# The values product of windowed attention split into quarters of the array

## The chip, the cores and the metric

The kernel runs on one core of one Trainium2 chip. The metric is the time of one execution on the device, in microseconds (us). TensorE does the matrix products, VectorE (DVE) and ScalarE (ACT) work on elements, GpSimd (POOL) does a few small things, SyncE (SP) issues the transfers.

## The reference

Three layers in a row, all in float32, for 4 sequences of 576 tokens, 8 heads of 64 (512 features):

```python
scores = scale * q @ k.T + slopes * -(pos_q - pos_k)      # per head
mask = (rel >= 0) & (rel < 128)                           # causal, a window of 128
attn = softmax(where(mask, scores, -1e9)) ;  x = attn @ v # 2304 x 512
h = x @ w_in ;  x = (h * clip(h + 3, 0, 6) / 6) @ w_out   # 512 -> 2048 -> 512
xn = x / rms(x) * rms_g
out = (silu(xn @ w_gate) * (xn @ w_val)) @ w_out2         # 512 -> 1536 -> 512
```

The window makes the attention local: a query tile of 128 sees keys of its own chunk of 128 and of the chunk before. In its own chunk query i sees keys 0 to i, in the one before it sees keys i+1 to 127.

## The kernel before

The 2304 tokens are 18 tiles of 128, in six blocks of three. Attention works on pairs of heads: for each block four pairs, 24 in all, and a pair has three steps, one for each query tile. The first feed-forward layer runs block by block; its inner loop (L710) has a slot for each of the 16 chunks of the hidden features. Work of the attention of the next block is laid into these slots by a table of offsets (L448 to L462), all in one program order that is written out by hand; each engine goes through its own instructions strictly in that order.

In every slot TensorE does product1 (L496, 12 matmuls into the one bank `ps_h`) and product2 of the slot before (L509, 9 matmuls). On `ps_h` ScalarE does the add-and-relu (L734), VectorE the min-and-multiply (L735), ScalarE the high part of the result (`g`, L744), VectorE the rest (L755). The next slot's product1 writes the same bank, so it waits for L735.

From the tenth pair on (`JOINT = 9`), a pair spreads over slots like this, pairs following each other every four slots:

- the scores slot: the scores of all three steps (L359, on quarters of the array), bias and maximum (L373, L380), exponentials (L388);
- the next slot: the divisions (L397, six on ScalarE) by the sums that POOL made. In the same slot stand the values of the pair before, so it is called the values slot here;
- the turn slot: VectorE transposes 32x32 blocks (L403), SyncE stores them to DRAM (L408);
- the fetch slot: SyncE loads them back in transposed order (L322);
- the next pair's scores slot: POOL selects what belongs to the chunk and to the one before (L423), into `pt`, 128 keys by two chunks by two heads by 128 queries. What the mask excludes is zero there;
- the next pair's values slot: the values product (L434).

The values product of a step is four matmuls of 128 keys by 64 features on 128 queries, for two chunks (`c`) and two heads (`a`), summed over the chunks in the bank `ps_av` (`sums_bank`). The first tile of a sequence that begins on a tile's edge has no chunk before it (`from_ = 1`) and takes two. Then `finish` (L327) moves the sum for all three steps to `xs`, the input of product1 one block later: ScalarE casts the high part (L335), VectorE subtracts for the low part (L336). After it SyncE is asked for the v of the pair after next (L310, two buffers).

In most slots of blocks three to five a unit of the second layer's weights is converted too (`W2.turn`, L219): L143, L133, L140 and at times L147 on VectorE, L136 and at times L145 on ScalarE, with loads (L203) and stores (L216) on SyncE.

The bank `ps_t` (`turned_bank`) takes transposes in the first nine pairs; later it only holds, with `ps_av`, the scores of the third step.

Of the kernel before, what the change touches and what calls it, by code (L numbers as in the profile page):

```python
# [11 lines left out]
F32R = mybir.dt.float32r  # L12
# [8 lines left out]
P = 128  # L21
B, H, S, D = 4, 8, 576, 64
# [3 lines left out]
KC = DM // P  # L26
# [20 lines left out]
JOINT = 9  # L47
# [21 lines left out]
def f32(ap):  # L69
    return ap.bitcast(F32)  # L70
# [3 lines left out]
def fused_kernel(ctx: ExitStack, tc: tile.TileContext, qd, kd, v, w1, w2, rms_g, out):  # L74
# [7 lines left out]
    vec, act, pool, pe, sp = nc.vector, nc.scalar, nc.gpsimd, nc.tensor, nc.sync  # L82
# [3 lines left out]
    xpool = ctx.enter_context(tc.tile_pool(name="xpool", bufs=2))  # L86
# [63 lines left out]
    def room(k, shape, dtype, name):  # L150
        return wpool.tile(shape, dtype, tag=f"w{k}", name=name)

    class First:
# [3 lines left out]
        def __init__(self):  # L157
            self.raw = [room(k, [P, 2 * DM], U64, "wraw") for k in range(M1)]
            self.loaded, self.runs, self.tiles = 0, [], []

        def load(self, upto):
            while self.loaded < min(upto, M1):
                sp.dma_start(out=self.raw[self.loaded], in_=w1[self.loaded])
                self.loaded += 1
# [116 lines left out]
    xs_of = {}  # L281
# [3 lines left out]
    turned_bank = ps_a.tile([P, 2, 2, P], F32, tag="T", name="ps_t")  # L285
# [3 lines left out]
    class Pair:  # L289


        def __init__(self, b, j):
            self.b, self.j = b, j
            self.i0, self.n = BLOCKS[b]
            self.lo = max(self.i0 - 1, 0)
            self.nch = self.i0 + self.n - self.lo
            self.acc = None
            self.plain = b * H // 2 + j in PLAIN

        def load(self):  # L300
            j, q0, nq, k0, nk = self.j, self.i0 * P, self.n * P, self.lo * P, self.nch * P
# [17 lines left out]
        def fetch(self):  # L319

            for k in range(0, P, 32):
                sp.dma_start(  # L322
                    out=weights_[k : k + 32, 1].rearrange("r u a (b s) -> r (u a b) s", s=32),
                    in_=self.d[:, :, :, k : k + 32].rearrange("u a (b r) s -> r (u a b) s", r=32),
                )

        def finish(self):  # L327

            nq = self.n * P
            x = self.acc.rearrange("p u q -> p (u q)")[:, :nq]  # L330
            if self.j == 0:
                xs = (x0pool if self.b == 0 else xpool).tile([P, KC, 2, 3 * P], F32R, tag="xs", name="xs")
                xs_of[self.b] = [xs[:, c] for c in range(KC)]
            t = xs_of[self.b][self.j]
            act.copy(t[:, 0, :nq], x)  # L335
            vec.tensor_sub(t[:, 1, :nq], x, f32(t[:, 0, :nq]))  # L336

    class Step:
# [89 lines left out]
        def values(self):  # L428
            pr = self.pair
            if pr.acc is None:  # L430
                pr.acc = sums_bank[:, :3]
            for c in range(self.from_, 2):
                for a in range(2):
                    pe.matmul(  # L434
                        pr.acc[a * D : (a + 1) * D, self.u],
                        lhsT=pr.vr[:, self.i - 1 + c - pr.lo, a * D : (a + 1) * D],
                        rhs=self.pt[:, c, a],
                        start=(c == self.from_),
                        stop=(c == 1),
                        skip_group_check=True,  # L440
                    )
# [8 lines left out]
    for k, pr in enumerate(pairs):  # L450
        b, j = divmod(k, H // 2)
# [12 lines left out]
    def at(t):  # L464
        return [slots[kind].get(t, []) for kind in KINDS]
# [8 lines left out]
                pairs[k].load()  # L474

    def finish(pr):
        pr.finish()
        k = pairs.index(pr) + 2
        if k < len(pairs):
            pairs[k].load_v()  # L480
# [108 lines left out]
    for t in range(AHEAD):  # L589
        q, s_, d_, t_, _, v_, _, _, _ = at(t)  # L590
# [46 lines left out]
    class Inputs:  # L637
# [19 lines left out]
        def sum(self, which, on, out):  # L657
            setattr(self, which, out)
            x, sub = self.block, on.tensor_sub
            if which == "S1":  # L660
                on.tensor_add(out, x(1, 0), x(1, 1))
            elif which == "S2":
                sub(out, self.S1, x(0, 0))
            elif which == "S3":
                sub(out, x(0, 0), x(1, 0))
            else:
                sub(out, x(0, 1), self.S2)
# [27 lines left out]
    for p, (b, m0, m1) in enumerate(PARTS):  # L695
        n = BLOCKS[b][1]
        last = p == len(PARTS) - 1
        nq = n * P
# [10 lines left out]
        xs = xs_of[b]  # L709
        for m in range(m0, m1):  # L710
            t, slot = slot, slot + 1
            q, s_, d_, t_, l_, v_, p_, r_, w_ = at(t)
# [37 lines left out]
                if m + 1 < CUT:  # L750
                    W1.step(m + 1, 3)
            for x in v_:
                if x.last:
                    finish(x.pair)
            vec.tensor_sub(g[:, 1, :nq], r[:, :nq], f32(g[:, 0, :nq]))  # L755
            for x in s_[2:]:
                x.bias()
            for x in s_:
# [13 lines left out]
                finish1(go)  # L772
            for x in l_:
                x.transpose()
            for x in d_:
                if x.via:
                    x.divide()
# [56 lines left out]
    acc = room(SUMS[0], [P, 4, DM], F32, "y"), room(SUMS[1], [P, 2, DM], F32, "y")  # L834
    acc = [acc[t // 4][:, t % 4] for t in range(6)]
# [29 lines left out]
    def group(i):  # L865
# [42 lines left out]
        if i + 3 not in ring and i + 3 not in parts:  # L908
            fetch(i + 3)
# [134 lines left out]
```

## Time and profile before

| | us |
|---|---|
| median of 3 runs | 930.15 (929.33 to 930.58) |
| the profiled execution | 929.06, of it the span 927.4 |
| TensorE busy | 912.2 (98% of the span) |
| VectorE busy | 634.8 (68%) |
| ScalarE busy | 456.0 (49%) |
| POOL busy | 181.6 (20%) |

The span runs from the first to the last instruction. Attention and first layer take its first 500 us or so, the second layer the rest. A matmul's end is modelled, so TensorE's busy time is no measure of how well it is used; starts are better. Every idle time of another engine is harmless unless TensorE waits behind it.

### The profile page before, as it was taken

How to read it: one execution, taken by the hardware profiler on the slowest of the kernel's cores; microseconds unless marked ns; L12 is line 12 of the kernel's file. 1: busy time of each engine (PE TensorE's matmuls, PEld its weight loads, DVE VectorE, ACT ScalarE, POOL GpSimd, SP SyncE). 2: the span in 40 equal slices, each digit the busy share in tenths (PEclk: the TensorE clock that was granted, in tenths of full speed). 3: DMA queues.
4: the chain of work that ended last, by engine and by line, in shares of the span. 5: the costliest groups of instructions: out<-in, count | busy, mean ns of one | idle time of the engine just before them, and what ended most of it. 6: DMA issues, size and time to landing. Idle time of an engine off the chain costs nothing.

```text
span 927.4 us, 15033 instructions
## 1 busy us (share of the span) xinstructions
PE 912.2 (98%) x5384; PEld 811.0 (87%) x5384; DVE 634.8 (68%) x1282; ACT 456.0 (49%) x994; POOL 181.6 (20%) x327
## 2 busy tenths in 40 slices
PE   7899999999999999999999999999999999999998
PEld 4588888888888888888999999999999999999997
DVE  5799666556887777886577667787545577545555
ACT  6899566565657656655455453423232223231120
POOL 4332013232234322332243322200000000000000
PEclk9999999999999999999999999999999999999999
DMA  7456412346998888884565788685757555755521
GB/s 241 173 212 224 168 40 67 77 86 186 257 276 236 221 226 227 206 211 116 158 216 220 270 263 309 244 288 204 276 207 276 209 204 205 276 209 209 209 88 68
DMA packets 156522, 186.84 MB, mean 201 GB/s; under 512 B 90528, under 2 KB 129952, under 8 KB 152096
## 3 DMA queue, kind: packets, MB, share of 16 engines
q1 hardware_dynamic: 156448, 185.89, 62.2%
q8 instruction: 42, 0.69, 0.3%
q14 instruction: 32, 0.26, 0.1%
HBM read 135.92 MB, written 49.94 MB: 200 GB/s over the span
## 4 chain that ended last, share of the span: by engine, by line
PE 94%; DVE 2%; ACT 2%; issue 1%; POOL 1%; POOLq 0%; ACTq 0%; DVEq 0%
PE ps_o L509 22%; PE ps_h L496 21%; PE ps_y L931 15%; PE ps_o L879 10%; PE ps_S L879 8%; PE ps_A L879 6%; PE ps_h L879 4%; PE ps_av L434 3%; PE ps_s L359 2%; PE ps_t L414 1%; ACT t L388 1%; PE ps_t L359 1%; PE warm L585 0%; DVE y L939 0%; DVE t L373 0%
## 5 line engine op out<-in xcount | busy, mean ns | idle before, releaser
L509 PE MATMUL ps_o<-w,g 128*128 128x512 f32 x864 | 219.7, 398 | 0.0
L496 PE MATMUL ps_h<-xs,w 128*128 128x384 f32 x1152 | 218.7, 338 | 0.7 <-DVE t L735 0.6
L496 PEld LDWEIGHTS ps_h<-xs,w 128*128 128x128 f32 x1152 | 204.1, 188 | 10.2 <-DVE t L735 2.8
L509 PEld LDWEIGHTS ps_o<-w,g 128*128 128x128 f32 x864 | 157.7, 188 | 38.6 <-issue 6.7
L931 PE MATMUL ps_y<-wo,g 128*128 128x512 f32 (+1 forms) x654 | 150.0, 387 | 0.0
L931 PEld LDWEIGHTS ps_y<-wo,g 128*128 128x128 f32 x654 | 121.9, 188 | 24.0
L735 DVE SCALAR_TENSOR_TENSOR t<-t,ps_h 128x384 f32<-128x384 f32 x96 | 53.1, 553 | 75.9 <-ACT t L734 75.7
L734 ACT ACTIVATE t<-ps_h,three 128x384 f32<-128x384 f32 x96 | 55.3, 576 | 72.2 <-PE ps_h L496 67.5
L939 DVE TENSOR_TENSOR y<-y,ps_y 128x512 f32<-128x512 f32 (+1 forms) x91 | 61.7, 679 | 34.2 <-PE ps_y L931 33.9
L744 ACT CAST g<-t 128x384 fp32r<-128x384 f32 x96 | 49.3, 514 | 56.9 <-DVE t L735 55.7
L388 ACT ACTIVATE t<-t,m 128x128 f32<-128x128 f32 (+1 forms) x144 | 61.2, 426 | 31.6 <-DVE t L380 23.6
L755 DVE TENSOR_TENSOR g<-t,g 128x384 fp32r<-128x384 f32 x96 | 55.9, 582 | 20.4 <-ACT g L744 19.7
L902 ACT ACTIVATE r<-r 128x384 f32<-128x384 f32 x36 | 18.9, 525 | 103.4 <-DVE r L901 103.4
L879 PE MATMUL ps_o<-S,tw 128*128 128x384 f32 x336 | 66.2, 339 | 0.0
L423 POOL TENSOR_SCALAR_AFFINE_SELECT pt<-pt 128x256 f32<-128x256 f32 x82 | 38.1, 479 | 125.4 <-DMA pt<-pd 122.6
L879 PEld LDWEIGHTS ps_o<-S,tw 128*128 128x128 f32 x336 | 59.3, 188 | 1.0 <-DVE u L890 0.8
L391 POOL TENSOR_TENSOR r<-r,minus 128x2 f32<-128x2 f32 x72 | 54.3, 754 | 6.0
L887 ACT COPY s<-ps_S 128x384 f32<-128x384 f32 x18 | 8.6, 479 | 85.0 <-PE ps_S L879 84.8
L143 DVE SCALAR_TENSOR_TENSOR wx<-wx,wy 128x512 uint32<-128x512 uint32 (+1 forms) x52 | 44.0, 846 | 0.0
L390 POOL TENSOR_SCALAR r<-den 128x2 f32<-128x2 f32 x72 | 23.4, 324 | 103.9 <-ACT t L388 100.1
L136 ACT ACTIVATE wx<-wraw 128x512 f32<-128x512 f32 (+1 forms) x52 | 42.7, 821 | 0.9 <-DVE w L147 0.9
L434 PE MATMUL ps_av<-pt,vraw 128*64 128x128 f32 x544 | 39.6, 285 | 0.2
(138 smaller groups left out, 1425.4 us busy)
## 6 DMA issues: line engine op xcount, KB each, us to landing
tw<-t SPq DMA_DIRECT2D x52, 896.0 KB, 6.3
wraw<-w SPq DMA_DIRECT2D x36, 512.0 KB, 4.2
wo<-w SPq DMA_DIRECT2D x18, 1024.0 KB, 5.0
wraw<-w SPq DMA_DIRECT2D x16, 1024.0 KB, 8.7
t<-th SPq DMA_DIRECT2D x12, 896.0 KB, 4.6
t<-tl SPq DMA_DIRECT2D x12, 896.0 KB, 5.0
b<-wx SPq DMA_DIRECT2D x24, 256.0 KB, 4.4
w<-w SPq DMA_DIRECT2D x12, 512.0 KB, 3.0
```

What stands on the lines that cost most here:

```text
L388: act.activation(p, p, AF.Exp, bias=self.m[:, a : a + 1], scale=-1.0, accum_out=self.den[:, a : a + 1])
L391: pool.tensor_tensor(self.r, self.r, minus, ALU.pow)
L434: pe.matmul(pr.acc[a * D : (a + 1) * D, self.u], lhsT=pr.vr[:, self.i - 1 + c - pr.lo, a * D : (a + 1) * D], rhs=self.pt[:, c, a], start=( ...
L496: pe.matmul(ps[:, : n * P], lhsT=w[:, a, c * P : (c + 1) * P], rhs=xs[c][:, b, : n * P], start=(k == 0), stop=(k == 3 * KC - 1),)
L509: pe.matmul(o, lhsT=g[:, a, i * P : (i + 1) * P], rhs=w[:, b], start=(m == first and a == 0 and b == 0), stop=(m == last and b == 1),)
L734: act.activation(r[:, :nq], ps[:, :nq], AF.Relu, bias=three)
L735: vec.scalar_tensor_tensor(out=r[:, :nq], in0=r[:, :nq], scalar=6.0, in1=ps[:, :nq], op0=ALU.min, op1=ALU.mult)
L744: act.copy(g[:, 0, :nq], r[:, :nq])
L755: vec.tensor_sub(g[:, 1, :nq], r[:, :nq], f32(g[:, 0, :nq]))
L879: pe.matmul(ps, lhsT=w[a][:, k, c * P : (c + 1) * P], rhs=x[:, b, c], start=(start and j == 0), stop=(j == 5), skip_group_check=True,)
L931: pe.matmul(ps[:, cols], lhsT=gs[i + k][:, a, t // 3, t % 3 * P : (t % 3 + 1) * P], rhs=wo[i + k][:, b, cols], start=(k == 0 and a == 0 an ...
L939: vec.tensor_add(acc[t][:, cols], acc[t][:, cols], ps[:, cols])
```

## The change

For pairs from the tenth on (`via`), the values product takes 64 keys at a time: keys 0 to 63 on the upper half of the array's rows into `ps_av`, keys 64 to 127 on the lower half into `ps_t`. For each half, one chunk is needed for all 128 queries (`whole`) and the other for 64 queries only; the quarter of each chunk that the mask leaves zero is not computed. A step has eight matmuls, four on 128 columns and four on 64, instead of four on 128 (a step without a chunk before it: four on 128 instead of two).

The result lies in two banks. `sum` copies the one to SBUF on ScalarE (into v's tile, which has been read), adds the other on VectorE, and casts the high part on ScalarE; `rest` subtracts for the low part on VectorE. `sum` is called after L755, `rest` and the request for the next v after product2, ahead of the divisions.

```diff
--- before.py
+++ after.py
@@ -296,6 +296,7 @@
             self.nch = self.i0 + self.n - self.lo
             self.acc = None
             self.plain = b * H // 2 + j in PLAIN
+            self.via = b * H // 2 + j >= JOINT
 
         def load(self):
             j, q0, nq, k0, nk = self.j, self.i0 * P, self.n * P, self.lo * P, self.nch * P
@@ -323,6 +324,23 @@
                     out=weights_[k : k + 32, 1].rearrange("r u a (b s) -> r (u a b) s", s=32),
                     in_=self.d[:, :, :, k : k + 32].rearrange("u a (b r) s -> r (u a b) s", r=32),
                 )
+
+        def sum(self):
+
+            nq = self.n * P
+            x, y = (bank.rearrange("p u q -> p (u q)")[:, :nq] for bank in (self.acc, self.acc_high))
+            if self.j == 0:
+                xs = xpool.tile([P, KC, 2, 3 * P], F32R, tag="xs", name="xs")
+                xs_of[self.b] = [xs[:, c] for c in range(KC)]
+            t = xs_of[self.b][self.j]
+            self.total = self.vr.rearrange("p c d -> p (c d)")[:, :nq]
+            act.copy(self.total, y)
+            vec.tensor_add(self.total, x, self.total)
+            act.copy(t[:, 0, :nq], self.total)
+
+        def rest(self):
+            nq, t = self.n * P, xs_of[self.b][self.j]
+            vec.tensor_sub(t[:, 1, :nq], self.total, f32(t[:, 0, :nq]))
 
         def finish(self):
 
@@ -429,7 +447,22 @@
             pr = self.pair
             if pr.acc is None:
                 pr.acc = sums_bank[:, :3]
-            for c in range(self.from_, 2):
+                pr.acc_high = turned_bank.rearrange("p c a q -> p (c a) q")[:, :3]
+            for whole in (True, False) if self.via else ():
+                for h, acc in enumerate((pr.acc, pr.acc_high)):
+                    rows = slice(h * D, (h + 1) * D)
+                    c = 1 if self.from_ else 1 - h if whole else h
+                    cols = slice(0, P) if whole else rows
+                    for a in range(2) if whole or not self.from_ else ():
+                        pe.matmul(
+                            acc[a * D : (a + 1) * D, self.u, cols],
+                            lhsT=pr.vr[rows, self.i - 1 + c - pr.lo, a * D : (a + 1) * D],
+                            rhs=self.pt[rows, c, a, cols],
+                            start=whole,
+                            stop=not whole or self.from_ == 1,
+                            skip_group_check=True,
+                        )
+            for c in range(self.from_, 2) if not self.via else ():
                 for a in range(2):
                     pe.matmul(
                         pr.acc[a * D : (a + 1) * D, self.u],
@@ -474,7 +507,10 @@
                 pairs[k].load()
 
     def finish(pr):
-        pr.finish()
+        if pr.via:
+            pr.rest()
+        else:
+            pr.finish()
         k = pairs.index(pr) + 2
         if k < len(pairs):
             pairs[k].load_v()
@@ -750,9 +786,12 @@
                 if m + 1 < CUT:
                     W1.step(m + 1, 3)
             for x in v_:
-                if x.last:
+                if x.last and not x.via:
                     finish(x.pair)
             vec.tensor_sub(g[:, 1, :nq], r[:, :nq], f32(g[:, 0, :nq]))
+            for x in v_:
+                if x.last and x.via:
+                    x.pair.sum()
             for x in s_[2:]:
                 x.bias()
             for x in s_:
@@ -772,6 +811,9 @@
                 finish1(go)
             for x in l_:
                 x.transpose()
+            for x in v_:
+                if x.last and x.via:
+                    finish(x.pair)
             for x in d_:
                 if x.via:
                     x.divide()
```

ScalarE in a values slot, in the kernel before, from the high part of `g` to the next slot's add-and-relu:

```order
L744 CAST g<-t 128x384
L335 CAST xs<-ps_av 128x384
L397 ACTIVATE t<-t,r 128x128 x6
L145 CAST w<-wx 128x512
L136 ACTIVATE wx<-wraw 128x512
L734 ACTIVATE t<-ps_h,three 128x384
```

and in the changed kernel, where later lines have moved on by 18 to 36 (L744 is now L780, L397 L415, L734 L770):

```order
L780 CAST g<-t 128x384
L337 COPY vraw<-ps_t 128x384
L339 CAST xs<-vraw 128x384
L415 ACTIVATE t<-t,r 128x128 x6
L145 CAST w<-wx 128x512
L136 ACTIVATE wx<-wraw 128x512
L770 ACTIVATE t<-ps_h,three 128x384
```

A copy of the bank `ps_t` stands ahead of the cast to `xs`, and that cast reads the sum in v's tile; the six divisions come behind both.

VectorE in a values slot, in the kernel before, from the min-and-multiply to the transposes of the turn slot:

```order
L735 SCALAR_TENSOR_TENSOR t<-t,ps_h 128x384
L336 TENSOR_TENSOR xs<-ps_av,xs 128x384
L755 TENSOR_TENSOR g<-t,g 128x384
L143 SCALAR_TENSOR_TENSOR wx<-wx,wy 128x512
L133 TENSOR_SCALAR wy<-wraw 128x512
L140 TENSOR_SCALAR wy<-wraw 128x512
L147 TENSOR_TENSOR w<-wx,w 128x512
L735 SCALAR_TENSOR_TENSOR t<-t,ps_h 128x384
L403 STREAM_TRANSPOSE t<-t 128x2x128 x3
```

and in the changed kernel (L735 is now L771, L755 L791, L403 L421):

```order
L771 SCALAR_TENSOR_TENSOR t<-t,ps_h 128x384
L791 TENSOR_TENSOR g<-t,g 128x384
L338 TENSOR_TENSOR vraw<-ps_av,vraw 128x384
L343 TENSOR_TENSOR xs<-vraw,xs 128x384
L143 SCALAR_TENSOR_TENSOR wx<-wx,wy 128x512
L133 TENSOR_SCALAR wy<-wraw 128x512
L140 TENSOR_SCALAR wy<-wraw 128x512
L147 TENSOR_TENSOR w<-wx,w 128x512
L771 SCALAR_TENSOR_TENSOR t<-t,ps_h 128x384
L421 STREAM_TRANSPOSE t<-t 128x2x128 x3
```

The low part of `g` has moved ahead of the work on `xs`, and an addition that reads `ps_av` and v's tile stands in front of the subtraction.

## Rows read from the trace of the kernel before

**Rows 1.** The page, chain that ended last, share of the span by engine.
```profile
PE 94%; DVE 2%; ACT 2%; issue 1%; POOL 1%; POOLq 0%; ACTq 0%; DVEq 0%
```

**Rows 2.** Timeline, TensorE: start us, us, engine, line, operation, tiles, shapes, count, idle before.
```profile
378.01 1.53 PE L434 MATMUL ps_av<-pt,vraw 128*64 128x128 f32 x24
379.47 2.33 PE L509 MATMUL ps_o<-w,g 128*128 128x512 f32 x9
...
385.83 2.27 PE L496 MATMUL ps_h<-xs,w 128*128 128x384 f32 x12
```

**Rows 3.** Timeline, VectorE, the same slots.
```profile
381.26 0.56 DVE L336 TENSOR_TENSOR xs<-ps_av,xs 128x384 fp32r<-128x384 f32 x1 [0.96 <-ACT xs L335]
381.73 0.55 DVE L755 TENSOR_TENSOR g<-t,g 128x384 fp32r<-128x384 f32 x1
...
384.62 0.56 DVE L735 SCALAR_TENSOR_TENSOR t<-t,ps_h 128x384 f32<-128x384 f32 x1 [0.21 <-ACT t L734]
```

**Rows 4.** Chain of waits from 282 us: start us, us, what.
```profile
290.83 0.44 DVE t L735
291.28 0.04 issue
```

**Rows 5.** Timeline, TensorE, third step of a scores stage.
```profile
274.12 0.27 PE L359 MATMUL ps_t<-kraw,qraw 64*64 64x128 f32 x1
...
274.14 0.32 PE L359 MATMUL ps_av<-kraw,qraw 64*64 64x192 f32 x1
274.23 0.27 PE L359 MATMUL ps_t<-kraw,qraw 64*64 64x128 f32 x1
...
274.30 0.32 PE L359 MATMUL ps_t<-kraw,qraw 64*64 64x192 f32 x1
```

**Rows 6.** Timeline, ScalarE, the slots of rows 2.
```profile
380.33 0.51 ACT L744 CAST g<-t 128x384 fp32r<-128x384 f32 x1 [0.62 <-DVE t L735]
380.75 0.47 ACT L335 CAST xs<-ps_av 128x384 fp32r<-128x384 f32 x1
381.12 1.87 ACT L397 ACTIVATE t<-t,r 128x128 f32<-128x128 f32 x6
...
383.44 0.68 ACT L136 ACTIVATE wx<-wraw 128x512 f32<-128x512 f32 x1
384.03 0.56 ACT L734 ACTIVATE t<-ps_h,three 128x384 f32<-128x384 f32 x1
```

**Rows 7.** L887 and L890: duration ns min/median/max, first and last start, form.
```profile
L887 ACT COPY s<-ps_S x18: 471/480/483, 517.3 to 901.5; 128x384 f32<-128x384 f32 x18
...
L890 DVE TENSOR_TENSOR u<-s,ps_A x18: 547/555/555, 508.9 to 895.2; 128x384 f32<-128x384 f32 x18
```

**Rows 8.** Timeline, ScalarE, turn slots, first and last of a kind; then one without idle.
```profile
166.71 0.58 ACT L734 ACTIVATE t<-ps_h,three 128x384 f32<-128x384 f32 x1 [0.99 <-ACT t L397]
...
305.12 0.58 ACT L734 ACTIVATE t<-ps_h,three 128x384 f32<-128x384 f32 x1 [0.49 <-PE ps_h L496]
...
344.56 0.58 ACT L734 ACTIVATE t<-ps_h,three 128x384 f32<-128x384 f32 x1 [0.55 <-PE ps_h L496]
...
422.69 0.68 ACT L136 ACTIVATE wx<-wraw 128x512 f32<-128x512 f32 x1
423.44 0.58 ACT L734 ACTIVATE t<-ps_h,three 128x384 f32<-128x384 f32 x1
...
441.84 0.58 ACT L734 ACTIVATE t<-ps_h,three 128x384 f32<-128x384 f32 x1 [1.49 <-PE ps_h L496]
```

**Rows 9.** Timeline, TensorE, product1 of two scores slots.
```profile
271.13 2.36 PE L496 MATMUL ps_h<-xs,w 128*128 128x384 f32 x12 [0.57 <-DVE t L735]
...
370.29 0.51 PE L496 MATMUL ps_h<-xs,w 128*128 128x384 f32 x2
```

**Rows 10.** Timeline, VectorE, ahead of the second of these.
```profile
369.55 0.54 DVE L735 SCALAR_TENSOR_TENSOR t<-t,ps_h 128x384 f32<-128x384 f32 x1
```

**Rows 11.** Timeline, POOL, the selects ahead of the values of rows 2.
```profile
375.59 3.00 POOL L423 TENSOR_SCALAR_AFFINE_SELECT pt<-pt 128x256 f32<-128x256 f32 x6 [2.44 <-DMA pt<-pd]
```

## The prediction

> **What bounds the kernel now.** I read the chain of waits first: 94% of the span goes through TensorE [rows 1]. So time moves only where TensorE's own work gets shorter or where TensorE is made to wait. The timeline of TensorE over one pair's four slots comes next [rows 2]: in the values slot the products L434 take 1.46 us, from 378.01 to 379.47, in which nothing else runs on TensorE; from there to 385.83 there is no printed idle. Then the timelines of ScalarE and VectorE beside it, because product1 (L496) has one PSUM bank and each of its slots waits until L734 and L735 have read the slot before. How near they are to being late is read there: VectorE's L735 of the turn slot runs from 384.62 for 0.56 [rows 3], to 385.18; where TensorE does wait for such an L735 it starts 0.04 after its end [rows 4]; so the bank was free for the fetch slot at 385.22 and TensorE came at 385.83 [rows 2]. That is 0.61 us of slack, and it is the number that decides this change.
>
> **What TensorE gains.** In the third step of a scores stage four products on 64 rows and 64 columns of the array start within 0.02, from 274.12 to 274.14, two more between these rows; the next on the same quarter comes 0.11 later after 128 streamed columns (274.23) and 0.16 later after 192 (274.30) [rows 5]. So four quarters of the array do run side by side, and 64 columns fewer make 0.05 less: I take 0.06 for a wave of four with 64 columns (bounds 0.05, and 0.11, as if it were no shorter than one with 128). The program's one f32 product is two records in the trace. A full step before is four products in two column halves, four waves of 0.11, 0.44 us; three such steps are 1.32 of the 1.46. After, it is two waves with 128 columns and two with 64: 0.34. It saves 0.10 a step. A step at the start of a sequence has no chunk before it and saves nothing. There are 15 pairs from the tenth on; 11 have three full steps (0.30), the four of the block that starts a sequence have two (0.20): 11 x 0.30 + 4 x 0.20 = 4.1 us at most, if nothing else moves (0 to 4.9 by the bounds).
>
> The Trainium skill speaks against the half waves: "TensorE: Matmul & The Clock Gate", section "Wait — 56ns, not 53.3ns?", has starts never closer than about 25 ns, however few the columns. By that a wave of four would last 100 ns, an estimate from that page, and the 4.1 would be 0.8. Here the trace disagrees: the four starts of [rows 5] lie within 20 ns.
>
> **What the eviction costs.** Before, in the values slot, ScalarE does L744, then L335 (0.47, the next 0.37 after its start), then six divisions L397 at 381.12, weight conversion up to L136, and L734 of the turn slot at 384.03, each as soon as the one before lets it [rows 6]. VectorE runs L336 ahead of L755 [rows 3]. After, by the order of instructions, ScalarE has a copy of the second bank, then the cast of the sum, and only then the divisions; VectorE has L755's subtraction first, then the addition, then the last subtraction.
> Step by step from L744 at 380.33: the copy starts at 380.75, as L335 did, and takes 0.48 [rows 7], to 381.23. L755 starts when L744 ends (380.84 + 0.02) at 380.86; as in [rows 3], where L755 comes 0.47 after L336, VectorE's next starts 0.47 on, at 381.33, and the addition takes 0.555 [rows 7], to 381.89. The cast starts at 381.91 and, like L744, lets the next start 0.42 on: the divisions begin at 382.33 instead of 381.12. ScalarE is held 1.21 us longer, of which 0.68 it stands waiting for the addition. I bound this by 0.4 (the cast alone, with no wait) and 1.4 (0.1 more for each of two handovers from engine to engine). The fourth instruction, VectorE's last subtraction, delays the weight conversion behind it by some 0.7, but L735 of the turn slot waits longer for ScalarE, so it costs nothing.
>
> **What TensorE then waits for.** L734 of the turn slot is delayed by 1.21 less the idle that ScalarE had ahead of it, L735 with it, and TensorE by that less the 0.61. (An instruction lets the next start about 0.1 before its own end, as L335 does, so 0.1 is added to a printed idle.) The 15 turn slots fall into four kinds.
> - Idle of 0.99 to 1.49 printed, four slots, first and last in [rows 8]: delay at most 0.12, nothing waits, TensorE keeps its gain: 3 x 0.30 + 0.20 = 1.1 us faster.
> - Idle of 0.49 to 0.55, three slots, first and last in [rows 8]: delay 0.6, just the slack. TensorE comes 0.30 early and waits it out: 0.
> - Idle of 0 to 0.15, five slots. One is that of 384.03, no idle: 1.21 - 0.61 = 0.60 later. Four are like 422.69 + 0.68 to 423.44, 0.07 idle [rows 8]: delay 1.0, 0.40 later each. Together 2.2 us.
> - Three slots where the chain from L735 of the turn slot through VectorE's queue is already what TensorE waits for, or nearly, one or two slots on. At 271.13 it waits 0.57 for L735 [rows 9], and at 291.32 the chain of waits has L735 right ahead of it [rows 4]; both follow turn slots without idle, so all 1.21 comes through, twice. At 370.29 [rows 9] it came 0.16 after L735 let it (369.55 + 0.54 + 0.04) [rows 10], and the delay is 1.0: 0.85. Together 3.3 us.
> In eight fetch slots (three and five) TensorE now stops where it did not; product1 after such a stop takes 2.36 against 2.27 [rows 2, 9]: 8 x 0.09 = 0.7.
> Sum: -1.1 + 0 + 2.2 + 3.3 + 0.7 = 5.1 us slower. The profiled execution took 929.06 (927.4 of it the span), so 934.2 by its clock; the median of the runs shown is 1.1 above it, and I forecast 935.2.
>
> Costed at nothing: v's tile is held until the last subtraction, and on SyncE its reload waits for that, some 2 us later than now. Behind it stands one load of raw weights, used two turns on, some 8 us (378.01 to 385.83 [rows 2]). The v reload itself is for the pair after next. If this cover were gone, L136 would wait for its DMA.
>
> **The rivals.**
> 1. The eviction is hidden and the gain stays, faster. The place is ScalarE ahead of L734 in the turn slot. For it speaks that four slots have the idle; against it, eight have less than 0.16. It decides from a hold of 0.4 down: then two kinds of the four keep their gain whole, the five nearly, and only the last three lose 0.8; that is 2.4 us faster, and with no hold at all 4.1, so 926.0 to 927.8. Chance 6%.
> 2. The hold is nearer 0.8. Then the five lose 0.2 in all, the last three 0.8 + 0.8 + 0.45, the stops 0.5, against 1.1 and 0.9 gained in the first two kinds: 0.8 us slower, 930.9, no change. Chance 12%.
> 3. POOL's selects become the wait. They run from 375.59 to 378.59 [rows 11]; the third step's product needed them at 378.01 + 2 x 0.44 = 378.89 and will at 378.69. Transposes later by 1.2, with TensorE later by 0.6, bring them 0.6 later, past that. The wait of 0.5 in the values slot mostly takes the place of the one in the fetch slot, so it costs nothing until the DMA round trip adds some 0.4 more; then 0.3 in eleven slots, 938.5. Chance 8%.
> 4. Half waves no shorter than full ones: the four slots that keep a gain keep none, 936.3. Chance 4%. The Trainium skill's 25 ns between starts, of the page named above, would stand behind this one.
>
> **How the numbers follow.** The forecast has 70%; its own range, from 0.1 us more or less hold in eleven slots and the unknown stops, is 932.5 to 938. With rivals 2 to 4 taken in, 930.8 to 938.8 leaves out under two in ten. A measurement of this kernel tells 0.2%, 1.9 us, from no change. Faster by that: rival 1 and a little, 7%. Within: rival 2 and the low end of the forecast, 14%. Slower: 79%.
>
> **What would show it.** In the changed trace: L734's counterpart in turn slots 0.1 to 1.2 later after its values slot; ScalarE idle some 0.7 ahead of the new cast, ended by VectorE's addition; TensorE's product1 in most fetch slots of 300 to 430 us with 0.5 to 0.9 idle, released by the min-and-multiply on VectorE; the values products in about 1.15 us instead of 1.46. I am wrong if the divisions start less than 0.8 after where they did, if fetch slots show no such idle, or if the values take as long as before.

## The result, and the profile after

The changed kernel takes 935.23 us (median of 6 runs, 933.41 to 937.95), the kernel before in the same comparison 930.26 us (median of 6, 929.33 to 930.58). The ratio is 1.0054, with a 95% interval of 1.0043 to 1.0065: the change makes the kernel 5 us slower. I had forecast 935.2.

The profiled execution took 935.2 us, 933.5 of it the span (before: 929.06 and 927.4). The chain of waits on the page shows where to look: TensorE's share has fallen from the 94% of [rows 1], VectorE and ScalarE have gone from 2% each to 7% and 6%, and DMAs have entered the chain.

```profile
PE 79%; DVE 7%; ACT 6%; DMA 3%; issue 3%; POOL 2%; SPq 1%; POOLq 0%; ACTq 0%; DVEq 0%
```

TensorE's waits in the changed kernel (engine, tile, line, releaser: us in total, times, longest) name the place: product1 (L532) now waits for the min-and-multiply (L771) in seven places. In the kernel before, the product1 row was 0.6 us, once.

```profile
PE ps_h L532 <- DVE t L771: 3.3, 7, 0.7
...
PE ps_av L457 <- POOL pt L441: 0.4, 2, 0.3
```

Next the four slots of [rows 2] again, on TensorE (timeline: start us, us, engine, line, operation, tiles, shapes, count, idle before).

```profile
382.41 0.33 PE L457 MATMUL ps_av<-pt,vraw 64*64 64x128 f32 x2
382.43 0.33 PE L457 MATMUL ps_t<-pt,vraw 64*64 64x128 f32 x2
382.57 0.28 PE L457 MATMUL ps_av<-pt,vraw 64*64 64x128 f32 x2
382.58 0.28 PE L457 MATMUL ps_t<-pt,vraw 64*64 64x128 f32 x2
382.68 0.22 PE L457 MATMUL ps_av<-pt,vraw 64*64 64x64 f32 x2
...
382.74 0.22 PE L457 MATMUL ps_av<-pt,vraw 64*64 64x64 f32 x2
...
382.80 0.28 PE L457 MATMUL ps_av<-pt,vraw 64*64 64x128 f32 x2
...
383.57 2.35 PE L545 MATMUL ps_o<-w,g 128*128 128x512 f32 x9
385.76 2.27 PE L532 MATMUL ps_h<-xs,w 128*128 128x384 f32 x12
387.87 2.25 PE L545 MATMUL ps_o<-w,g 128*128 128x512 f32 x9
390.65 2.38 PE L532 MATMUL ps_h<-xs,w 128*128 128x384 f32 x12 [0.53 <-DVE t L771]
```

The values last 1.16 us (382.41 to 383.57) in place of 1.46. After a wave of 128 columns the next comes 0.11 later (382.57 to 382.68), after one of 64 columns 0.06 later (382.68 to 382.74, 382.74 to 382.80). Two slots on, TensorE has to stop for 0.53 us. What it waits for is read on ScalarE and VectorE. ScalarE first, to be held against [rows 6]:

```profile
384.53 0.52 ACT L780 CAST g<-t 128x384 fp32r<-128x384 f32 x1 [0.62 <-DVE t L771]
384.95 0.47 ACT L337 COPY vraw<-ps_t 128x384 f32<-128x384 f32 x1
386.17 0.51 ACT L339 CAST xs<-vraw 128x384 fp32r<-128x384 f32 x1 [0.74 <-DVE vraw L338]
386.58 1.87 ACT L415 ACTIVATE t<-t,r 128x128 f32<-128x128 f32 x6
...
389.44 0.57 ACT L770 ACTIVATE t<-ps_h,three 128x384 f32<-128x384 f32 x1
```

The divisions start 2.05 us after the high cast of g (386.58 - 384.53); in [rows 6] it was 0.79 (381.12 - 380.33). ScalarE is held 1.26 us, 0.74 of it waiting for the addition; over the 14 slots that have divisions the hold is 1.23 to 1.27. VectorE, against [rows 3]:

```profile
385.08 0.59 DVE L791 TENSOR_TENSOR g<-t,g 128x384 fp32r<-128x384 f32 x1 [0.58 <-ACT g L780]
385.59 0.55 DVE L338 TENSOR_TENSOR vraw<-ps_av,vraw 128x384 f32<-128x384 f32 x1
386.71 0.56 DVE L343 TENSOR_TENSOR xs<-vraw,xs 128x384 fp32r<-128x384 f32 x1 [0.58 <-ACT xs L339]
...
390.04 0.56 DVE L771 SCALAR_TENSOR_TENSOR t<-t,ps_h 128x384 f32<-128x384 f32 x1 [0.35 <-ACT t L770]
```

The min-and-multiply of the turn slot ends at 390.60, and TensorE starts at 390.65. Before, the bank had been free 0.61 us before TensorE came.

Not all of the 6.1 us between the two spans is the change's. Product1 of the first slot, long before any changed instruction, already starts 1.45 us later. The windows of the start show what goes with it (window, us; busy us and count of TensorE, its weight loads, VectorE, ScalarE, POOL; granted clock, DMA share, GB/s). Before, and then after:

```profile
0.00:20.00 20.00, 14.43 (x104) 8.72 (x104) 10.93 (x57) 12.45 (x37) 8.37 (x25) 0.91 0.80 267
20.00:40.00 20.00, 15.03 (x148) 9.68 (x148) 14.74 (x55) 16.32 (x47) 8.96 (x19) 0.91 0.33 99
```

```profile
0.00:20.00 20.00, 15.21 (x98) 8.92 (x98) 10.15 (x54) 11.80 (x34) 8.40 (x25) 0.83 0.78 266
20.00:40.00 20.00, 15.51 (x143) 9.45 (x144) 14.93 (x58) 16.05 (x48) 8.76 (x17) 0.83 0.29 91
```

The mean granted clock of the first 40 us was 0.91 before and 0.83 after, so TensorE, which has gaps there, ran for longer at the lower of its two levels (1.2 and 2.4 GHz) in the one execution than in the other. The 14 traces of this case, with the same instructions up to the first changed values slot, fall into two groups: product1 of that slot starts at 158.25 to 159.07 us where the clock of the first 40 us was 0.91, and at 159.44 to 160.00 where it was 0.79 to 0.83. So I compare traces only from the first changed values slot (158.3 us in the trace before) to the last turn slot. There the change costs 4.62 us. All sums "in the stretch" below are these, taken from the starts of product1, one profiled execution of each kernel.

### The profile page after: what moved, and what is told of

Same layout as the page of the kernel before. It is cut to its first block, busy times and chain, and to the rows that moved or that the text cites. A ratio compares the mean times of both kernels' runs of the same rounds, so it can differ in the third digit from the quotient of the medians.

```text
span 933.5 us, 15778 instructions
## 1 busy us (share of the span) xinstructions
PE 915.6 (98%) x5728; PEld 809.6 (87%) x5728; DVE 643.9 (69%) x1297; ACT 462.5 (50%) x1009; POOL 182.3 (20%) x327
## 4 chain that ended last, share of the span: by engine, by line
PE 79%; DVE 7%; ACT 6%; DMA 3%; issue 3%; POOL 2%; SPq 1%; POOLq 0%; ACTq 0%; DVEq 0%
PE ps_h L532 16%; PE ps_y L973 15%; PE ps_o L545 15%; PE ps_o L921 10%; PE ps_S L921 8%; PE ps_A L921 6%; PE ps_h L921 4%; PE ps_s L377 1%; PE ps_av L467 1%; DVE t L391 1%; DMA pt<-pd 1%; PE ps_t L432 1%; POOL pt L441 1%; ACT t L415 1%; DVE t L771 1%
## 5 line engine op out<-in xcount | busy, mean ns | idle before, releaser
L532 PE MATMUL ps_h<-xs,w 128*128 128x384 f32 x1152 | 220.3, 339 | 3.7 <-DVE t L771 3.3
L532 PEld LDWEIGHTS ps_h<-xs,w 128*128 128x128 f32 x1152 | 203.3, 188 | 17.1 <-DVE t L771 9.6
L771 DVE SCALAR_TENSOR_TENSOR t<-t,ps_h 128x384 f32<-128x384 f32 x96 | 53.1, 553 | 67.7 <-ACT t L770 67.1
L770 ACT ACTIVATE t<-ps_h,three 128x384 f32<-128x384 f32 x96 | 55.2, 575 | 62.2 <-PE ps_h L532 61.4
L780 ACT CAST g<-t 128x384 fp32r<-128x384 f32 x96 | 49.4, 515 | 56.6 <-DVE t L771 54.8
L791 DVE TENSOR_TENSOR g<-t,g 128x384 fp32r<-128x384 f32 x96 | 55.3, 576 | 29.1 <-ACT g L780 28.5
L409 POOL TENSOR_TENSOR r<-r,minus 128x2 f32<-128x2 f32 x72 | 56.8, 789 | 6.0
L136 ACT ACTIVATE wx<-wraw 128x512 f32<-128x512 f32 (+1 forms) x52 | 42.6, 820 | 0.0
L948 DVE TENSOR_TENSOR t<-t,r 128x768 f32<-128x768 f32 x36 | 34.5, 959 | 3.8
```

What stands on the lines that cost most here:

```text
L409: pool.tensor_tensor(self.r, self.r, minus, ALU.pow)
L532: pe.matmul(ps[:, : n * P], lhsT=w[:, a, c * P : (c + 1) * P], rhs=xs[c][:, b, : n * P], start=(k == 0), stop=(k == 3 * KC - 1),)
L770: act.activation(r[:, :nq], ps[:, :nq], AF.Relu, bias=three)
L771: vec.scalar_tensor_tensor(out=r[:, :nq], in0=r[:, :nq], scalar=6.0, in1=ps[:, :nq], op0=ALU.min, op1=ALU.mult)
L780: act.copy(g[:, 0, :nq], r[:, :nq])
```

## The experiments

Two theories stood against each other at first. H: the cost is ScalarE's hold in the values slot, which reaches TensorE through the turn slot's relu, and it hides the products' gain. P: the products themselves, in quarters and over two banks, bring nothing.

**products_alone.** The old `finish` at its old place, from the first bank; `sum` and `rest` not called. It leaves the second bank, half of the keys, out of the result.

```
...
             for x in v_:
-                if x.last and not x.via:
+                if x.last:
                     finish(x.pair)
...
```

> The changed kernel's products over halves of the keys, but the eviction of the kernel before, at its old place: one ScalarE cast and one VectorE subtraction, from the first bank only. The second bank is written and never added, so half of the keys is missing from the sums. Theory (the products pay, the eviction costs): the values slot is 0.30 us shorter in eleven pairs and 0.20 in four, and nothing is held; 4.1 us faster at most, and less where TensorE then meets a wait that was hidden: 926 to 927.5 us, and the fetch slots show no wait of product1 that the kernel before did not have. Rival (the products in quarters cost as much as they save, by the second bank or by the half waves): the time stays at 930 and the values take 1.46 us as before.

928.51 us against 930.44, ratio 0.9982 (0.9972 to 0.9991). P falls. In the stretch it is 2.36 us faster: 0.14 to 0.29 in each of 14 pairs, 3.06 together, and 0.70 slower in one. The theory's 4.1 was an upper bound. In the slow pair the second and the third step of the values wait for POOL's selects (TensorE, timeline), and the values take 2.16 us:

```profile
417.06 0.33 PE L457 MATMUL ps_av<-pt,vraw 64*64 64x128 f32 x2 [0.27 <-POOL pt L441]
...
417.90 0.33 PE L457 MATMUL ps_av<-pt,vraw 64*64 64x128 f32 x2 [0.27 <-POOL pt L441]
```

**products_full.** The same with the zero quarter put back (half of the keys is left out here too).

```
...
-                    cols = slice(0, P) if whole else rows
+                    cols = slice(0, P)
...
```

> The kernel with the products alone (row halves, two banks, the eviction of the kernel before from the first bank only, so half of the keys is missing from the sums), and with the zero quarter put back: every product has 128 columns, four waves a step. Theory (a wave lasts 0.11 us for 128 columns and 0.06 for 64, and the row halves by themselves change nothing): the values take 1.46 us again and the gain is gone, 930 to 930.8. Rival (the quarters of the array do it, whatever the columns): as with the products alone, 928 to 929.

931.23 us against 930.18, ratio 1.0017 (1.0008 to 1.0026); 0.58 slower in the stretch, a little more than expected. Every wave now has 128 columns and lasts 0.11 (380.15 to 380.26); the values start at 379.77, and what follows them 1.48 later, at 381.25 (TensorE, timeline).

```profile
379.77 0.33 PE L457 MATMUL ps_av<-pt,vraw 64*64 64x128 f32 x2
...
380.15 0.28 PE L457 MATMUL ps_av<-pt,vraw 64*64 64x128 f32 x2
...
380.26 0.28 PE L457 MATMUL ps_av<-pt,vraw 64*64 64x128 f32 x2
...
381.25 0.97 PE L542 MATMUL ps_o<-w,g 128*128 128x512 f32 x3
```

So all of the products' gain is the zero quarter; row halves and two banks by themselves give none.

**eviction_alone.** The changed eviction, with the old products and a bank for each chunk.

```
-            for whole in (True, False) if self.via else ():
-                for h, acc in enumerate((pr.acc, pr.acc_high)):
...
+            for h, acc in enumerate((pr.acc, pr.acc_high)) if self.via else ():
+                rows = slice(h * D, (h + 1) * D) if self.from_ else slice(0, P)
+                c = 1 if self.from_ else h
...
```

> The kernel with the new eviction (copy, addition, cast, subtraction, in the new places) and the four products of the kernel before, over all 128 keys: the chunk before goes to the one bank, the chunk itself to the other. Only the first step of a sequence, which has one chunk, is cut into row halves, so that both banks hold something. Theory: TensorE gains nothing and ScalarE is held 1.26 us in each of the 15 pairs, so the whole cost shows, 5.1 + 1.1 = 6.2 us by the prediction's sum, less the 1.1 us that one of its slots turned out not to pay: 935.3 to 936.5. Rival (the time of the changed kernel comes from the quarters and not from the eviction): 930 to 931.

936.27 us against 930.44, ratio 1.0062 (1.0050 to 1.0074), 5.34 slower in the stretch. The eviction is the whole cost; the products give back 0.72 of it (5.34 to 4.62) where alone they gain 2.36. Up to 0.6 of the 5.34 belongs to this kernel's own products: in the four pairs that begin a sequence the values take 1.40 us in place of 1.24.

**dose1, dose2, dose3.** The kernel before with n more copies on ScalarE.

```
             act.copy(t[:, 0, :nq], x)
+            for _ in range(n if self.b * H // 2 + self.j >= JOINT else 0):
+                act.copy(self.vr.rearrange("p c d -> p (c d)")[:, :nq], x)
```

> The kernel before with one more ScalarE copy of 128x384 from PSUM behind the cast of the eviction, in the 15 pairs from the tenth on. In the run with three of them the divisions started 1.41 us later, so one is a hold of 0.47. Theory (the hold decides, and the prediction's idle times and 0.61 us of slack say from where): twelve of the slots take 0.47 for nothing, only the three in which VectorE's queue is already what TensorE waits for pay, 0.47 + 0.47 + 0.1, and two stops of 0.09: 1.2 us slower, 931.6. Rival (each hold is paid in proportion, a third of the three copies' 8.3 us): 2.8 us slower, 933.2.

> The same with two copies, a hold of 0.94. Theory: the three slots with about half a microsecond of idle pay nothing, five pay 0.33 + 4 x 0.16, three pay 0.94 + 0.94 + 0.58, and the stops 0.7: 4.1 us slower, 934.5. Rival (in proportion): 5.5 us slower, 935.9.

> The kernel before with three more ScalarE copies of 128x384 from PSUM behind the cast of the eviction in the 15 pairs from the tenth on (they write v's tile, which nobody reads any more): 3 x 0.42 = 1.26 us of hold on ScalarE and no wait in it, no work on VectorE, and the products as they were. Theory (the hold of ScalarE ahead of the next slot's relu is all that matters): by the prediction's four kinds of slots 0 + 3 x 0.05 + (0.65 + 4 x 0.45) + (1.26 + 1.26 + 0.9) + 8 x 0.09 = 6.7 us slower, 937; 5.4 if the slot near 270 us does not pay, 935.7. Rival (what costs is the wait between ScalarE and VectorE and back, or VectorE's longer queue, not the length of the hold): under 932.

Measured 931.83 (ratio 1.0014, 1.0006 to 1.0023), 934.09 (1.0047, 1.0034 to 1.0060) and 938.33 (1.0092, 1.0079 to 1.0105); in the stretch 1.2, 3.5 and 8.3 us slower. A hold of ScalarE with no wait and no VectorE work in it is enough to make the kernel slow, and the cost bends as the idle times and the slack said. The holds were not the 0.47, 0.94 and 1.26 of the expectations: the divisions start 0.37, 0.89 and 1.40 us later, and these cost 1.2, then 2.2 more, then 4.8 more. With the holds as measured the prediction's working gives 2 x 0.37 + 2 x 0.09 = 0.9, then 0.28 + 4 x 0.07 + (0.89 + 0.89 + 0.52) + 0.7 = 3.6, and 3 x 0.19 + (0.79 + 4 x 0.58) + (1.40 + 1.40 + 1.03) + 0.7 = 8.2: right to 0.3 us in the sum, though not kind by kind (the table below).

**total_in_pt.** The sum goes into pt, so that v's reload need not wait.

```
-            self.total = self.vr.rearrange("p c d -> p (c d)")[:, :nq]
+            self.total = weights_[:, 0].rearrange("p u a q -> p (u a q)")[:, :nq]
```

> The changed kernel with one edit: the sum of the two banks is written into the half of the weights' tile pt that the products have just read, and not into v's tile. So the reload of v on SyncE waits only for the products, as in the kernel before, and no longer for VectorE's last subtraction. Theory (the prediction's: this reload and what stands behind it on SyncE is hidden, all of the cost is the hold on ScalarE): no change against the changed kernel, 934.5 to 936. Rival (the later reload holds the stores and loads of the turned weights behind it, and some of the cost is there): 932 to 934.

934.92 us against 930.42, ratio 1.0048 (1.0033 to 1.0062): as the changed kernel, as expected (3.88 slower in the stretch, against 4.62). But TensorE comes to it by other waits, which the expectation did not have: 2.5 us for POOL's selects, and 0.6 for the min-and-multiply.

```profile
PE ps_av L457 <- POOL pt L441: 2.5, 8, 0.8
PE ps_h L532 <- DVE t L771: 0.6, 2, 0.4
```

So the time is as forecast; that it is the same hold in the same place is not shown by this run, and why the selects come late here is open.

**cast_on_vector.** The wait is taken from ScalarE.

```
-            act.copy(t[:, 0, :nq], self.total)
+            vec.tensor_copy(t[:, 0, :nq], self.total)
```

> The changed kernel with one edit: the cast of the sum is done by VectorE, behind its own addition, so ScalarE has only the copy, which takes the place of the old cast, and goes straight on to the divisions. ScalarE's hold is 0, VectorE has 0.5 us of cast more. Theory: the gain of the products comes through, 4.1 us, less what VectorE's queue (about 0.9 us longer in this slot than before, with 0.2 us idle at its end) takes back in the slots where it is what TensorE waits for, 3 x 0.3: 926.5 to 928. Rival (it is VectorE's longer queue that delays the min-and-multiply): no better than the changed kernel, 935 to 937.

932.66 us against 930.44, ratio 1.0032 (1.0021 to 1.0043). Better than the changed kernel by 2.6 (1.87 slower in the stretch, against 4.62), so the hold was a large part of the cost; but far from the gain that I expected, and neither side of the expectation has the reason. TensorE waits 0.2 us for the min-and-multiply, and 2.1 us for POOL's selects:

```profile
PE ps_av L457 <- POOL pt L441: 2.1, 7, 0.5
...
PE ps_h L532 <- DVE t L771: 0.2, 1, 0.2
```

The turned weights go from VectorE to DRAM, back, and through POOL's selects to the values product. In [rows 11] this path had 0.3 us to spare (378.59 against 378.89). Here it comes round late, and then, as I read it, it feeds itself: the selects delay POOL's reciprocals behind them, these the divisions of the next pair, and these the next turn. The divisions wait for the reciprocals in ten places, which they never do in the kernel before (ScalarE's waits, then its timeline):

```profile
ACT t L415 <- POOL r L409: 7.2, 10, 1.0
```

```profile
342.31 0.69 ACT L415 ACTIVATE t<-t,r 128x128 f32<-128x128 f32 x2 [0.55 <-POOL r L409]
344.03 0.70 ACT L415 ACTIVATE t<-t,r 128x128 f32<-128x128 f32 x2 [1.03 <-POOL r L409]
```

**sum_on_pool.** Cast and last subtraction on POOL.

```
-            act.copy(t[:, 0, :nq], self.total)
+            pool.tensor_copy(t[:, 0, :nq], self.total)
...
-            vec.tensor_sub(t[:, 1, :nq], self.total, f32(t[:, 0, :nq]))
+            pool.tensor_sub(t[:, 1, :nq], self.total, f32(t[:, 0, :nq]))
```

> The changed kernel with the last two steps of the eviction, the cast of the sum and the subtraction, on POOL, which has nothing to do at that point. ScalarE has one copy, as long as the old cast and in its place; VectorE has one addition, as long as the old subtraction. So neither is held. Theory (the changed kernel is slow by the hold of ScalarE and, with the cast on VectorE, by VectorE's longer queue): the products' gain comes through as in the kernel with the products alone, 926.5 to 928.5. Rival (with the sums right, something else holds it: POOL's two steps delay the reload of v, or the selects come late all the same): 930 to 933.

945.25 us against 930.40, ratio 1.0160 (1.0138 to 1.0182): outside both. POOL comes to the cast only after its selects and reciprocals (POOL, timeline):

```profile
390.55 0.86 POOL L409 TENSOR_TENSOR r<-r,minus 128x2 f32<-128x2 f32 x1
391.37 0.50 POOL L339 CAST xs<-vraw 128x384 fp32r<-128x384 f32 x1
391.95 1.02 POOL L343 TENSOR_TENSOR xs<-vraw,xs 128x384 fp32r<-128x384 f32 x1
```

and v's reload waits on SyncE for it, from the store before it to 393.00, with the store of the turned weights behind it (SyncE, timeline):

```profile
384.03 0.53 SPq L216 DMA_DIRECT2D b<-wx  x1
393.00 0.39 SPq L311 DMA_DIRECT2D vraw<-v  x1
393.48 0.46 SPq L203 DMA_DIRECT2D wraw<-w  x1
394.03 0.38 SPq L216 DMA_DIRECT2D w<-w  x1
394.66 3.03 SPq L426 DMA_DIRECT2D pd<-t  x3
```

**pool_and_pt.** The same with the sum in pt, and the fourth pair of a block, whose sums are needed at once, on VectorE.

```
+            self.total = weights_[:, 0].rearrange("p u a q -> p (u a q)")[:, :nq]
...
+            (vec if self.j == 3 else pool).tensor_copy(t[:, 0, :nq], self.total)
...
+            (vec if self.j == 3 else pool).tensor_sub(t[:, 1, :nq], self.total, f32(t[:, 0, :nq]))
```

> The same with the cast and the last subtraction moved as well: to POOL in the three pairs of a block whose sums are not needed at once, to VectorE in the fourth. ScalarE has one copy in the old cast's place, VectorE one addition in the old subtraction's, POOL 1.5 us more behind its reciprocals; the reload of v waits for none of it. In the run with both steps on POOL and the sum in v's tile, the reload was issued 5.7 us later than in the changed kernel, 393.0 against 387.3, and the selects came late for it. Theory (that reload was what cost the 15 us there, and without a hold the products' gain comes through): 926.5 to 929. Rival (POOL itself is late: its selects and reciprocals, and the divisions behind them, cost whatever the place of the sum): 933 to 945.

931.52 us against 930.42, ratio 1.0009 (1.0000 to 1.0018): 13.7 us better than sum_on_pool. Two things differ, the place of the sum and the fourth pair's move to VectorE; but of the 13.0 us between the two in the stretch 9.8 lie in the eleven pairs that stay on POOL in both, so v's reload was most of that kernel's loss. But pool_and_pt lies between the theory and the rival: TensorE waits 2.4 us for selects in 7 places.

**v_load_early.** The same with v's load ahead of the slot's stores again.

```
     def finish(pr):
-        if pr.via:
-            pr.rest()
-        else:
+        if not pr.via:
             pr.finish()
...
-                if x.last and not x.via:
+                if x.last:
                     finish(x.pair)
...
                 if x.last and x.via:
-                    finish(x.pair)
+                    x.pair.rest()
```

> The kernel with the sum in pt and its last steps on POOL, and with the load of v issued where the kernel before issues it, ahead of the stores of the slot. In the run without this edit the stores of the turned weights landed 2.5 us after their issue in the median and 5.8 at most (255 to 440 us), against 2.0 and 3.3 with the products alone, and TensorE waited 2.4 us for selects. Theory (the loads that were issued later lie on the DMA engines beside these stores): landing goes back to about 2.0, TensorE's waits for selects to under 1, but L136 waits for L147 again in the slot near 270 us, 0.7 to 1.0; in sum 929 to 930.5. Rival (the stores land late for another reason, so only the 0.7 to 1.0 is lost): 932 to 933.

931.98 us against 930.18, ratio 1.0020 (1.0011 to 1.0029). TensorE's waits for selects fell to 0.5 us, as the theory wanted, and L136 waits 0.90 us for L147 again; but the stores' median landing stayed at 2.6 us and the median time did not follow. The stretch of the profiled execution did, from 1.07 slower in pool_and_pt to 0.37 faster here, but at 930.80 that execution is the second fastest of eleven. Both expectations fail in a part. Why this kernel and pool_and_pt stay about 3 us above products_alone I have not settled.

**v_load_late.** The kernel before with v's load behind the slot's stores, and nothing else. It is for the one pair in which the prediction was most wrong.

```
-    def finish(pr):
-        pr.finish()
+    def load_v(pr):
         k = pairs.index(pr) + 2
         if k < len(pairs):
             pairs[k].load_v()
+
+    def finish(pr):
+        pr.finish()
+        if not pr.via:
+            load_v(pr)
...
+            for x in v_:
+                if x.last and x.pair.via:
+                    load_v(x.pair)
             for x in d_:
                 if x.via:
                     x.divide()
```

> The kernel before with one edit: in the pairs from the tenth on, SyncE issues the load of v behind the stores of the slot and not ahead of them, as the changed kernel does. No instruction of another engine moves. It is for the period from 256 to 277 us, where the changed kernel lost 0.07 us in place of the 1.21 that I had forecast. Theory (the new order of the DMAs changes which queue's count one weight conversion of ScalarE, L136, waits for; before it stands 0.90 us until VectorE's L147 has ended, after it does not): that conversion follows L145 at once, product1 no longer waits 0.57 in the slot at 271 us, and this period alone gets 0.7 to 1.0 us shorter; 929.5 in all. Rival (the wait went because the eviction shifted the work around it): the period stays as it was, 930.3.

929.18 us against 930.40, ratio 0.9989 (0.9980 to 0.9997). In the stretch two pairs change, by -0.81 and -0.67 us, and no other by more than 0.06. ScalarE in the slot near 270 us, in the kernel before and then in v_load_late (timeline):

```profile
267.82 0.63 ACT L145 CAST w<-wx 128x512 fp32r<-128x512 f32 x1 [1.53 <-DVE wx L143]
269.35 0.67 ACT L136 ACTIVATE wx<-wraw 128x512 f32<-128x512 f32 x1 [0.90 <-DVE w L147]
```

```profile
269.23 0.62 ACT L145 CAST w<-wx 128x512 fp32r<-128x512 f32 x1 [1.53 <-DVE wx L143]
269.76 0.68 ACT L136 ACTIVATE wx<-wraw 128x512 f32<-128x512 f32 x1
```

The wait is gone, here as in all six others with v's load behind the stores (the changed kernel, eviction_alone, total_in_pt, cast_on_vector, sum_on_pool, pool_and_pt), and it is there in all seven with the load ahead of them (the kernel before, products_alone, products_full, the three doses, v_load_early). In the traces this instruction waits for one DMA's semaphore and for VectorE's in the kernel before, and for two DMA semaphores in v_load_late, where only DMAs were moved. Of the versions that compute the whole result this is the only one faster than the kernel before, by 0.1%.

## Why the prediction was right, step by step

- **TensorE's gain.** 0.30 a pair in the values slot: measured 1.46 to 1.16. The wave of 64 columns, 0.06, is in the rows above, and products_full shows that the whole gain hangs on it. The Trainium skill ("TensorE: Matmul & The Clock Gate", section "Wait — 56ns, not 53.3ns?") has starts no closer than about 25 ns; here the two banks' products, two each, start 0.02 apart in the first wave (382.41, 382.43) and 0.01 in the second (382.57, 382.58). The measurement decides, and rival 4 is out.
- **The hold.** Forecast 1.21, 0.68 of it waiting; measured 1.26 and 0.74. eviction_alone shows that the eviction is what costs, and the doses that a hold of this length is enough for it: on a straight line between the second and the third a hold of 1.24 costs 6.8 us; less the 1.4 that the move of v's load brings (v_load_late) that is 5.4, an estimate, and eviction_alone has 5.34 with its own products in it.
- **The slack of 0.61 and the four kinds of turn slots.** The periods from one values slot to the next, summed by kind:

| kind (pairs) | forecast us | changed kernel | eviction_alone | dose1 | dose2 | dose3 | products_alone |
|---|---|---|---|---|---|---|---|
| ScalarE idle 0.99 and more (4) | -1.1 | -0.49 | 0.22 | 0.24 | 0.03 | 0.03 | -0.78 |
| idle about half a us (3) | 0.27 | 0.40 | 0.52 | 0.22 | 0.04 | 0.83 | -0.84 |
| no idle (5) | 2.65 | 2.99 | 2.98 | 0.24 | 1.68 | 3.92 | -0.20 |
| VectorE's chain, from 256 us | 1.21 | 0.07 | -0.16 | -0.04 | 0.47 | 1.22 | -0.15 |
| from 277 us | 1.21 | 0.95 | 0.77 | 0.31 | 0.59 | 1.17 | -0.19 |
| from 356 us | 0.85 | 0.70 | 1.01 | 0.23 | 0.63 | 1.14 | -0.20 |
| sum | 5.1 | 4.62 | 5.34 | 1.21 | 3.45 | 8.31 | -2.36 |

  (The forecast's 8 stops of 0.09 are put with their kinds.) In the changed kernel the kinds stand within 0.6 of the forecast, all but the pair from 256 us. The doses bear out that the second kind hardly pays for a hold of 0.89 and pays for one of 1.40. The last three pairs do not pass a hold on whole: together 0.50, 1.69 and 3.53 for holds that would give 0.74, 2.30 and 3.83. That the first dose's sum was met is partly luck, since twelve pairs that were to pay nothing paid 0.7.
- **The sign in the fetch slots, met in part.** Of six between 300 and 430 us two had the wait forecast, 0.53 (at 390.65) and 0.58 (at 410.95). In three of the other four TensorE had been held up in the values slot already, by 0.1 to 0.6 us. Counted by starts of product1, the way from turn slot to fetch slot is 5.46 us longer in sum over all pairs, from fetch slot to scores slot 1.13, and the values slots 2.06 shorter.
- **The term that failed.** The pair from 256 us was to pass the whole delay through, 1.21, and paid 0.07. I had read its wait of 0.57 [rows 9] as VectorE's own chain. Behind it stood a wait of ScalarE's L136, and the change took that away by moving v's load behind the stores, a move that I had put at nothing. v_load_late shows it: that move alone is worth 0.81 in this pair and 0.67 in the next. How much of the 0.67 is left in the changed kernel is not shown, since that next pair still pays 0.95 there.
- **The gain that was kept.** 1.1 forecast in the first kind, 0.49 measured. The last of these pairs lost its gain: its values slot takes 5.89 us where 5.55 is usual, because the selects come late. That is rival 3, and it weighs more than the 0.4 us of printed waits: from 316 us on five pairs' values take 1.27 to 1.77 us in place of 1.16, 1.7 together. In the first of them the third step starts at 323.51, when the selects have run from 320.84 to 323.45 (TensorE and POOL, timelines):

```profile
323.51 0.33 PE L457 MATMUL ps_av<-pt,vraw 64*64 64x128 f32 x2 [0.27 <-POOL pt L441]
```

```profile
320.84 2.61 POOL L441 TENSOR_SCALAR_AFFINE_SELECT pt<-pt 128x256 f32<-128x256 f32 x6 [3.87 <-DMA pt<-pd]
```

  Most of it takes the place of the wait in the fetch slot, as the prediction said of this rival: in four of the five the pair as a whole stays within 0.25 of its forecast, and the last pays its 0.35 in full.
- **Costed at nothing: v's reload.** Its wait for the last subtraction was right at nothing, to within the 0.7 us by which total_in_pt is better in the stretch; its place behind the stores was not, as the term that failed shows. Nor was the wait without effect: from 255 to 440 us the stores of the turned weights land 1.9 us after their issue in the median before, 3.1 in the changed kernel, and 2.0 in total_in_pt. And in sum_on_pool, where the cover was gone, most of the 15 us lost hung on it, as far as pool_and_pt can tell.
- **The total.** 5.1 forecast, 4.62 in the stretch, and luck has a part in it, because the errors cancel: the hold alone was forecast at 5.1 + 1.1 = 6.2 and costs 6.8 by the doses, the products give back 0.72 and not 1.1, and the move of v's load, put at nothing, brings 1.4. That the median of 935.23 lies on the forecast itself is luck too: each kernel's runs spread over 1 to 5 us, of which the start alone makes 1.45 between the two profiled executions.

## What to carry to other kernels

Before you shorten the work of the engine that bounds a kernel, look at what its results are then put through: here 0.30 us less on TensorE brought 1.26 us on ScalarE, and the slack between them was 0.61. Price a hold by counting, slot by slot, the idle ahead of the next instruction that matters; the doses show that such a count can be right to 0.3 us in the sum, and almost a microsecond off for one kind of slot. A moved DMA can change waits on instructions that have nothing to do with it, so compare the waits of the whole program, not only those of the edited lines.

## What was not expected of the hardware

- The granted clock over the first 40 us differed from execution to execution with the same instructions there, 0.91 and 0.83 in these two, 0.79 to 0.91 over the 14 traces, and product1 of the first changed values slot moved with it, from 158.25 to 160.00 us.
- The same stores, of the same size, landed after 1.9 us in the median in one kernel and after 3.1 in another (4.3 in sum_on_pool, 6.7 at most). In the slot of [rows 2], the load of raw weights ahead of them was issued 5.5 us earlier in the kernel before (380.07 and 385.56) and 3.2 us earlier in the changed one (387.77 and 390.98). That this load makes them late is not shown: eviction_alone has the same 3.2 us there (387.45 and 390.65) and 2.3 in the median, and v_load_early has the early load and 2.6.
